# Reordering the load phase of a fused attention and gMLP kernel, and carrying waits to earlier matmuls

## The chip, the cores and the metric

The kernel runs on one core of one Trainium2 chip. The metric is the device time of one execution in microseconds. A kernel is run several times and the median is quoted. The chips and the executions differ by some microseconds (the kernel before took 866.45 us in the median of one call and 868.37 and 869.62 on another chip, its runs 865.66 to 870.82), so kernels are compared with the kernel before *of the same rounds on the same chip*. A ratio is the mean time of one kernel's fast runs over that of the other's of the same rounds, so it is not quite the ratio of the medians that stand beside it.

## The reference

A recurrent attention block (64 segments of 32 tokens; each segment sees 8 memory tokens that the one before produced) is followed by a gMLP block. Here only the start matters: the Q, K and V projections of tokens that do not depend on the recurrence.

```python
h = x + _A_ref(_layernorm(x), A_mem0, A_Wq, A_Wk, A_Wv, A_Wo, 32)   # x (1,2048,512), W (512,32,128)
# in _A_ref, for each of 64 segments:
h = concatenate([mem, xs]);  q, k, v = h@Wq, h@Wk, h@Wv
p = softmax(where(mask, q@k.T * scale, -1e9));  o = (p@v)@Wo
mem = o[:, :8];  outs.append(o[:, 8:])
# then
return h + _B_ref(_layernorm(h), B_w_in, B_w_sp, B_b_sp, B_w_out)
```

The projections of a segment's own 32 tokens do not depend on the memory tokens, and the kernel projects the last 8 tokens of every segment ahead, in chunks of 16 segments (128 tokens): chunks 0 and 1 in a *load phase* before segment 0, chunks 2 and 3 inside the segments.

## The kernel before

All engines' programs are written through an emitter that works out which semaphores each operation must wait for. A second wait of a matmul becomes an instruction of its own in PE's stream (221 semaphore instructions in the trace of the kernel before).

```python
def finalize(self):                       # (cut: dependencies -> waits, newest producer first)
    ...
            op.waits = waits
    ...
def emit(self, eng_name, eng, sems, dma_sems):
    for op in self.by_eng[eng_name]:
        for d in op.waits:
            ... eng.wait_ge(...)
        ins = op.fn(eng)
```

The loads, all from one queue (SP), in this order: the two x chunks (128 KB each), four Q weight pieces of 1 MB, three more x blocks. The V and K pieces (1 MB each, four of each) follow after the code below.

```python
    load_xe(0, 0)
    load_xe(1, 1)
    for hq in range(4):
        load_w(0, hq)
    load_x(0, 4); load_x(1, 5); load_xe(2, 6)          # (layout cut)
    ...
    def ln_stats(j):
        dve(bn_stats ...);  dve(bn_aggr ...)
        pool(tensor_scalar add EPS);  pool(tensor_tensor pow -0.5)      # (arguments cut)
    ...
    for j in range(2):
        ln_stats(j)
    for j in range(2):
        ln_apply(j)
        xT(j, 6 + j)            # four PE transposes
        xe_copy(j, 6 + j)       # one ACT copy of 128x512
```

The projection groups. A Q or K group is 16 matmuls of 128 columns (four heads), a V group 16 matmuls of 512 columns on quarter arrays; each goes to one of four PSUM banks in turn and is copied out by ACT or DVE. A V group's result goes to an SBUF buffer and from there to DRAM.

```python
    def vx_evac(ck, n, bank, eng="act"):
        if ck < 2:
            t, tok = part[:, n, :], [("part", n, 0), ("part", n, 1)]    # chunk 0 and chunk 1 share part[n]
        ...                                                           # copy to t, scaled
        sp(lambda e: e.dma_start(dst, ...t...), reads=tok, writes=[("vext", ck, n)])
    ...
    for i in range(8):                     # Q
        for ck in range(2): start_group(qkx_mm, qkx_evac, ck, i)
    for n in range(8):                     # V of chunk 0
        if n < 3: ln_apply(n + 4)
        start_v(0, n)
        if n == 1: xT(4, 6); ring_copy(0, 6)
        if n == 2: xT(5, 7); ring_copy(1, 7)
        if n == 3: xT(6, 6); xe_copy(2, 6); mem0_transpose(7); load_wo(0)
    load_wo(1)
    for j in range(2): load_vx(j)          # waits for chunk 0's stores
    for i in range(8, 12):  ...            # first half of K, both chunks
    for n in range(8):                     # V of chunk 1
        start_v(1, n)
        if n % 4 == 3: load_wo(2 + n // 4)
    for i in range(12, 16): ...            # second half of K
    # then the 64 segments
```

## Time and profile before

| | before |
|---|---|
| time, first rounds | 868.42 us (867.87 to 869.19) |
| profiled span | 866.1 us |
| PE busy | 849.6 us, 98% |
| first Q matmul | 7.82 us |
| Q groups end | 24.51 us |
| first half of K starts | 33.59 us |
| segment 0 starts | 55.12 us |

The page of the kernel before, its span and its busy rows (busy time of an engine, share of the span, instructions; then tenths of each of 40 slices):

```profile
span 866.1 us, 45456 instructions
PE 849.6 (98%) x22453; PEld 433.9 (50%) x18876; DVE 501.8 (58%) x1246; ACT 467.4 (54%) x1291; POOL 158.6 (18%) x427
PE   6999999999999999999999999999999999999998
DMA  9972232213141211222241313342211690032101
```

PE is the limit almost everywhere; only the first slice has room. DMA is full in the first two slices and most of the third, to about 60 us: that is the second limit of the load phase.

The timeline of the kernel before at its start (start in us, length in us, engine, line, operation, out<-in, shapes, count; in brackets the idle time before it and what ended that):

```profile
0.79 1.32 SPq L309 DMA_DIRECT2D f_xn<-in_A_x_dram  x2
2.16 2.69 SPq L315 DMA_DIRECT2D f_arena<-in_A_Wq_dram  x4
3.49 0.69 DVE L364 BATCH_NORM_STATS2 f_st<-f_xn 128x6 f32<-128x512 bf16 x1 [3.49 <-DMA f_xn<-in_A_x_dram]
5.40 0.41 DVE L374 TENSOR_SCALAR f_xn<-f_xn,f_mv,f_rs 128x512 bf16<-128x512 bf16 x1 [0.21 <-POOL f_rs L368]
7.82 16.37 PE L426 MATMUL f_ps<-f_hTe,f_arena 128*128 128x128 bf16 x249 [0.16 <-DMA f_arena<-in_A_Wq_dram]
```

The Q groups start when the first weight piece is there. By the records of the single matmuls, about 46 of them are 107 ns apart, until 12.7 us, and the rest 56 ns.

The PE timeline of the kernel before, the rest of the load phase:

```profile
24.51 1.91 PE L461 MATMUL f_ps<-f_arena,f_hTe 128*32 128x512 bf16 x32
26.90 0.40 PE L384 MATMUL f_ps<-f_ident,f_part 128*128 128x128 bf16 x4 [0.48 <-DVE f_part L374]
33.59 7.32 PE L426 MATMUL f_ps<-f_hTe,f_arena 128*128 128x128 bf16 x128
40.84 7.09 PE L461 MATMUL f_ps<-f_arena,f_hTe 128*32 128x512 bf16 x128
47.87 7.32 PE L426 MATMUL f_ps<-f_hTe,f_arena 128*128 128x128 bf16 x128
55.12 0.40 PE L280 MATMUL f_ps<-f_arena,f_hT 128*32 128x512 bf16 x4
```

From the first V group to segment 0, PE waits once, for 0.48 us.

### The profile page before, as it was taken

The numbers are of one execution on the slowest core, as the hardware profiler recorded it, in microseconds if no ns is written. First come the engines' busy times: TensorE is split into PE (matmuls) and PEld (weight loads), VectorE is DVE, ScalarE is ACT, GpSimd is POOL, SyncE is SP. The second block draws the span as 40 slices with busy tenths as digits, with TensorE's granted clock in tenths as the row PEclk, the third lists the DMA queues.
The fourth block names the chain that finished last, engine by engine and source line by source line (L and its number), as shares of the span: only waits on it lengthen the run. The fifth ranks groups of instructions, "written<-read, shape, count | busy, mean of one in ns | idle before, by whom it ended". The sixth has DMA issues, their size and how long they took to land.

```text
span 866.1 us, 45456 instructions
## 1 busy us (share of the span) xinstructions
PE 849.6 (98%) x22453; PEld 433.9 (50%) x18876; DVE 501.8 (58%) x1246; ACT 467.4 (54%) x1291; POOL 158.6 (18%) x427
## 2 busy tenths in 40 slices
PE   6999999999999999999999999999999999999998
PEld 6664445454445544455445554454554444444443
DVE  3446666666666666666666666566655564363343
ACT  3445666666666666666666666666666655400000
POOL 1621212121212212121211221121211122100000
PEclk9999999999999999999999999999999999999999
DMA  9972232213141211222241313342211690032101
GB/s 323 380 218 72 69 74 74 64 42 85 26 92 29 78 38 50 77 70 57 68 85 31 92 41 93 62 92 58 59 51 42 193 274 16 1 104 77 64 13 39
DMA packets 114180, 75.20 MB, mean 87 GB/s; under 512 B 70712, under 2 KB 99520, under 8 KB 113984
## 3 DMA queue, kind: packets, MB, share of 16 engines
q1 hardware_dynamic: 113840, 72.19, 30.4%
q8 instruction: 164, 2.69, 1.3%
q14 instruction: 32, 0.26, 0.1%
q10 hardware_dynamic: 144, 0.07, 0.0%
HBM read 39.46 MB, written 20.58 MB: 69 GB/s over the span
## 4 chain that ended last, share of the span: by engine, by line
PE 96%; DVE 2%; DMA 1%; issue 1%; SPq 0%; ACT 0%
PE f_ps L280 30%; PE f_ps L660 14%; PE f_ps L281 13%; PE f_ps L1092 11%; PE f_ps L426 3%; PE f_ps L710 3%; PE f_ps L461 3%; PE f_ps L1166 3%; PE f_ps L1054 3%; PE f_ps L574 3%; PE f_ps L1085 3%; PE f_ps L625 3%; PE f_ps L631 1%; PE f_ps L554 1%; PE f_ps L681 1%; DMA f_arena<-in_A_Wq_dram 1%
## 5 line engine op out<-in xcount | busy, mean ns | idle before, releaser
L280 PE MATMUL f_ps<-f_arena,f_hT 128*32 128x512 bf16 (+1 forms) x5120 | 352.8, 337 | 1.7 <-issue 0.5
L281 PE MATMUL f_ps<-f_arena,f_hT 128*32 128x256 bf16 (+1 forms) x3072 | 214.5, 308 | 0.0
L280 PEld LDWEIGHTS f_ps<-f_arena,f_hT 128*32 128x32 bf16 x5120 | 121.0, 96 | 168.8 <-issue 85.6
L518 ACT ACTIVATE f_Tst<-f_ps 128x512 bf16<-128x512 f32 (+1 forms) x320 | 149.9, 510 | 57.6 <-PE f_ps L280 53.9
L660 PE MATMUL f_ps<-f_arena,f_cT 128*32 128x256 bf16 x4096 | 134.6, 273 | 1.4 <-ACT f_cT L645 1.1
L597 POOL TENSOR_TENSOR f_E_sb<-f_R_sb,f_E_sb 128x64 bf16<-128x64 f32 x128 | 48.2, 377 | 378.5 <-ACT f_R_sb L589 378.5
L526 DVE STREAM_TRANSPOSE f_QT<-f_Tst 128x256 uint32<-128x256 uint32 x128 | 57.1, 446 | 94.9 <-ACT f_Tst L518 94.9
L660 PEld LDWEIGHTS f_ps<-f_arena,f_cT 128*32 128x32 bf16 x4096 | 92.7, 95 | 35.6 <-ACT f_cT L645 21.2
L1092 PE MATMUL f_ps<-f_arena 128*128 128x512 bf16 x448 | 100.6, 379 | 0.0
L617 DVE TENSOR_SCALAR f_V_sb<-f_ps 128x512 bf16<-128x512 f32 (+1 forms) x128 | 70.6, 551 | 41.1 <-PE f_ps L280 41.1
L672 ACT ACTIVATE f_part<-f_ps 128x256 bf16<-128x256 f32 x128 | 49.2, 384 | 68.2 <-PE f_ps L660 68.2
L647 DVE TENSOR_SCALAR f_cT<-f_ps 128x160 bf16<-128x160 f32 (+1 forms) x192 | 61.0, 373 | 38.0 <-PE f_ps L631 38.0
L645 ACT ACTIVATE f_cT<-f_ps 128x160 bf16<-128x160 f32 (+1 forms) x192 | 53.0, 348 | 38.9 <-PE f_ps L631 38.9
L1092 PEld LDWEIGHTS f_ps<-f_arena 128*128 128x128 bf16 x448 | 43.8, 98 | 52.7
L526 DVE STREAM_TRANSPOSE f_KT<-f_Tst 128x128 uint32<-128x128 uint32 (+1 forms) x192 | 66.0, 356 | 2.7
L585 ACT ACTIVATE f_R_sb<-f_ps 128x160 f32<-128x160 f32 x128 | 38.9, 304 | 33.5 <-PE f_ps L281 25.6
L1098 DVE TENSOR_TENSOR f_arena<-f_ps,f_arena 128x512 f32<-128x512 f32 x28 | 19.3, 689 | 54.4 <-PE f_ps L1092 52.4
L567 ACT ACTIVATE f_E_sb<-f_ps 128x224 bf16<-128x224 f32 x128 | 45.7, 357 | 0.1
L593 DVE TENSOR_TENSOR f_E_sb<-f_R_sb,f_E_sb 128x160 bf16<-128x160 f32 x128 | 44.7, 350 | 0.0
L589 ACT ACTIVATE f_R_sb<-f_R_sb 128x160 f32<-128x160 f32 x128 | 42.6, 333 | 2.0
L710 PE MATMUL f_ps<-f_arena,f_cTx 128*32 128x512 bf16 x512 | 40.6, 380 | 0.0
L280 PE MATMUL f_ps<-f_arena,f_hTe 128*32 128x512 bf16 x512 | 39.0, 382 | 0.0
(105 smaller groups left out, 1026.7 us busy)
## 6 DMA issues: line engine op xcount, KB each, us to landing
wT_d<-f_wst SPq DMA_DIRECT2D x32, 256.0 KB, 2.7
f_arena<-wT_d SPq DMA_DIRECT2D x32, 256.0 KB, 4.6
f_arena<-in_A_Wq_dram SPq DMA_DIRECT2D x4, 1024.0 KB
f_arena<-in_A_Wv_dram SPq DMA_DIRECT2D x4, 1024.0 KB
f_arena<-in_A_Wk_dram SPq DMA_DIRECT2D x4, 1024.0 KB, 16.0
f_arena<-in_A_Wo_dram SPq DMA_DIRECT2D x4, 1024.0 KB
f_Vx<-vext_d SPq DMA_DIRECT2D x128, 32.0 KB
f_xn<-in_A_x_dram SPq DMA_DIRECT2D x16, 128.0 KB, 2.7
```

The source lines that it names most:

```text
L280: return e.matmul(out, lhsT=lhsT, rhs=rhs, start=start, stop=stop, skip_group_check=True, tile_position=pos)
L281: return e.add_instruction(mybir.InstMatmult(name=nc.get_next_instruction_name(), engine=mybir.EngineType.PE, ins=[e.lower_ap(rhs), e.lowe ...
L518: act(lambda e: e.activation(out=st_.rearrange("p (hp i r) -> p hp i r", i=32, r=2), in_=ps[:, bank, 0:64 * np_].rearrange("p (hp r i) -> ...
L526: dve(lambda e: e.transpose(out=dst, in_=src), reads=tok, writes=[(nm, b, k) for k in halves(b, p0, np_)])
L597: pool(lambda e: e.tensor_tensor(out=ev, in0=rv, in1=ev, op=ALU.mult), reads=[("R", b), ("Ex", b)], writes=[("Ex", b)])
L617: dve(lambda e: e.tensor_scalar(out=dst, in0=src, scalar1=VSC, scalar2=None, op0=ALU.mult), reads=[PB(bank)], writes=tok)
L645: act(lambda e: e.activation(out=dst, in_=src, func=ACT.Copy, scale=UNSC), reads=[PB(PVB[c])], writes=tok)
L647: dve(lambda e: e.tensor_scalar(out=dst, in0=src, scalar1=UNSC, scalar2=None, op0=ALU.mult), reads=[PB(PVB[c])], writes=tok)
L660: pe(lambda e, h=h, g=g, i=i, b=b, c=c: e.matmul(ps[32 * g:32 * g + 32, bank, 0:d1 - d0], lhsT=cTh[:, i, 8:40], rhs=w_o[:, h, d0:d1], star ...
L672: act(lambda e: e.activation(out=part[:, s % 8, d0:d1], in_=ps[:, bank, 0:d1 - d0], func=ACT.Copy), reads=[PB(bank)], writes=[("part", s % ...
L710: pe(lambda e, h=h, g=g, i=8 * qr + bg: e.matmul(ps[32 * g:32 * g + 32, WXB, :], lhsT=cTx[:, rb % 2, i, :], rhs=w_o[:, h, :], start=(i < 4 ...
L1092: pe(lambda e: e.matmul(ps[:, bank, 0:TB], lhsT=z2[:, sc, fb * 128:(fb + 1) * 128], rhs=wTb[tb % 2][:, :, sc, :], start=(sc == 0), stop=(s ...
```

## The change

The intent is to start the Q groups sooner and with a warm array (the Q matmuls 56 ns apart from the first, not 107), to keep PE from running into the V and K weights, which come at the pace of DMA, and to rid PE of the separate wait instructions. The diff, cut to its core:

```diff
# finalize: a matmul's second wait is moved to the nearest earlier PE operation without one (at most 60 back, after the producer)
+        pe = self.by_eng["pe"]
+        for op in pe:
+            while len(op.waits) > 1:
+                d = op.waits[-1]
+                t = next((p for p in reversed(pe[max(0, op.pos - 60):op.pos]) if not p.waits and p.gidx > d.gidx), None)
+                if t is None:
+                    break
+                op.waits.pop()
+                t.waits = [d]
# loads: half a piece first; the second x chunk by ACT's queue
+        if mi == 0 and hq == 0:
+            cm = c0 + 4 * DH
+            sp(lambda e, c0=c0: e.dma_start(ws[:, :, c0:cm], wr[:, :, c0:cm]), writes=["W0"])
+            c0 = cm
+    load_xe(1, 1, "act")
     load_xe(0, 0)
-    load_xe(1, 1)
# chunk 1's first V groups get buffers of their own
-        if ck < 2:
+        if ck == 1 and n < 4:
+            t, tok = (hbuf, xo)[n // 2][:, n % 2, :], [(("h", "xo")[n // 2], n % 2)]
+        elif ck < 2:
# start: warming matmuls, 1/sqrt on ACT instead of POOL, copies in halves on ACT and DVE
-    for j in range(2):
-        ln_stats(j)
-    for j in range(2):
-        ln_apply(j)
-        xT(j, 6 + j)
-        xe_copy(j, 6 + j)
+    for _ in range(44):
+        pe(lambda e: e.matmul(ps[:, 1, 0:128], lhsT=onesrc[:, 0:128], rhs=onesrc[:, 0:128], start=True, stop=True), ...)
+    ln_bn(0)
+    ln_root(0)
+    ln_bn(1)
+    ln_apply(0)
+    ln_root(1)
+    xe_halves(0, 0, (6, 7))
+    ln_apply(1)
+    ...                               # first Q groups in halves, chunk 1's transposes between them
# V: half of chunk 1 between chunk 0's groups; the x transposes one V group of chunk 0 later
         start_v(0, n)
-        if n == 1:
+        if n % 2 == 1:
+            start_v(1, n // 2)
+        if n == 2:
             xT(4, 6)
...
-        if n == 3:
+        if n == 4:
             xT(6, 6)
             xe_copy(2, 6)
             mem0_transpose(7)
             load_wo(0)
...
-    for n in range(8):
+    for n in range(4, 8):
         start_v(1, n)
-        if n % 4 == 3:
-            load_wo(2 + n // 4)
+        if n % 2 == 1:
+            load_wo(n // 2)
```

More of the change, by code (lines that the diff above doesn't have):

```diff
@@ L305, in xbuf, with load_xe @@
         return (xn[:, j, :], [("xn", j)]) if j < 2 else (part[:, j, :], [("part", j, 0), ("part", j, 1)])
-    def load_xe(ck, j):
+    def load_xe(ck, j, q="sp"):
         t, tok = xbuf(j)
-        sp(lambda e: e.dma_start(t, xe[CK * ck:CK * ck + CK, XM:SEG, :]), writes=tok)
+        em.add(q, lambda e: e.dma_start(t, xe[CK * ck:CK * ck + CK, XM:SEG, :]), writes=tok, dma=True)
     def load_w(mi, hq):
@@ L314, in load_w @@
         c0, c1 = hq * 8 * DH, (hq + 1) * 8 * DH
+        if mi == 0 and hq == 0:
+            cm = c0 + 4 * DH
+            sp(lambda e, c0=c0: e.dma_start(ws[:, :, c0:cm], wr[:, :, c0:cm]), writes=["W0"])
+            em.mark_const("W0")
+            c0 = cm
         sp(lambda e: e.dma_start(ws[:, :, c0:c1], wr[:, :, c0:c1]), writes=[("W", mi, hq)])
         em.mark_const(("W", mi, hq))
+    load_xe(1, 1, "act")
     load_xe(0, 0)
-    load_xe(1, 1)
     for hq in range(4):
@@ L358, in late_consts, with ln_bn @@
         pool(lambda e: e.tensor_copy(out=mask[:, 224:448], in_=mask[:, 0:224]), reads=["mask"], writes=["mask"])
-    def ln_stats(j):
+    def ln_bn(j):
         t, tok = xbuf(j)
@@ L364, in ln_stats, with ln_root @@
         dve(lambda e: e.bn_stats(out=st1[:, k, :], in_=t), reads=tok, writes=[("st1", k)])
+    def ln_root(j):
+        k = j % 3
+        dve(lambda e: e.bn_aggr(out=mv1[:, k, :], in_=st1[:, k, :]), reads=[("st1", k)], writes=[("mv1", k)])
+        act(lambda e: e.activation(out=rs1[:, k:k + 1], in_=mv1[:, k, 1:2], func=ACT.Ln, bias=EPS), reads=[("mv1", k)], writes=[("rs1", k)])
+        act(lambda e: e.activation(out=rs1[:, k:k + 1], in_=rs1[:, k:k + 1], func=ACT.Exp, scale=-0.5), reads=[("rs1", k)], writes=[("rs1", k)])
+    def ln_stats(j):
+        k = j % 3
+        ln_bn(j)
         dve(lambda e: e.bn_aggr(out=mv1[:, k, :], in_=st1[:, k, :]), reads=[("st1", k)], writes=[("mv1", k)])
@@ L379, in ln_inplace, with xT @@
         ln_apply(j)
-    def xT(j, bank):
+    def xT(j, bank, dcs=range(DC)):
         t, tok = xbuf(j)
-        for dc in range(DC):
+        for dc in dcs:
             pe(lambda e, dc=dc: e.transpose(out=psb[:, bank, dc * 128:(dc + 1) * 128], in_=t[:, dc * 128:(dc + 1) * 128],
@@ L393, in x_flip @@
         sp(lambda e: e.dma_start(xs_d[i], t), reads=rd, writes=[("xs", i)])
-        sp(lambda e: e.dma_start_transpose(out=dst, in_=xs_d[i]), reads=[("xs", i)], writes=[tok])
+        sp(lambda e: e.dma_start_transpose(out=dst, in_=xs_d[i]), reads=[("xs", i)], writes=tok)
     def ring_fill(rb):
@@ L408, in xe_copy, with xe_halves @@
         src = psb[:, bank, 0:512].rearrange("p (dc c) -> p dc c", dc=DC)
-        act(lambda e: e.activation(out=hTe[:, ck % 3, :, :], in_=src, func=ACT.Copy), reads=[PB(bank)], writes=[("hTe", ck % 3)])
+        act(lambda e: e.activation(out=hTe[:, ck % 3, :, :], in_=src, func=ACT.Copy), reads=[PB(bank)],
+            writes=[("hTe", ck % 3, 0), ("hTe", ck % 3, 1)])
+    def xe_halves(ck, j, banks):
+        for hf in range(2):
+            xT(j, banks[hf], (2 * hf, 2 * hf + 1))
+        for hf in range(2):
+            src = psb[:, banks[hf], 256 * hf:256 * hf + 256].rearrange("p (dc c) -> p dc c", dc=2)
+            dst = hTe[:, ck, 2 * hf:2 * hf + 2, :]
+            if hf == 0:
+                act(lambda e, dst=dst, src=src: e.activation(out=dst, in_=src, func=ACT.Copy), reads=[PB(banks[0])], writes=[("hTe", ck, 0)])
+            else:
+                dve(lambda e, dst=dst, src=src: e.tensor_copy(out=dst, in_=src), reads=[PB(banks[1])], writes=[("hTe", ck, 1)])
     def mem0_transpose(bank):
@@ L417, in mem0_transpose, with qkx_mm @@
         act(lambda e: e.activation(out=hT[:, 0, :, 0:M], in_=src, func=ACT.Copy), reads=[PB(bank)], writes=[("hTm", 0, 0), ("hTm", 0, 1)])
-    def qkx_mm(ck, i, bank):
+    def qkx_mm(ck, i, bank, hhs=range(4)):
         mi, q = i // 8, i % 8
         ws = (w_q, w_k)[mi]
-        for hh in range(4):
+        for hh in hhs:
+            wt = "W0" if i < 2 and hh < 2 else ("W", mi, q // 2)
             h = 8 * (q // 2) + 2 * hh + q % 2
@@ L427, in qkx_mm @@
                                                          rhs=hTe[:, ck % 3, dc, :], start=(dc == 0), stop=(dc == DC - 1)),
-                   reads=[("hTe", ck % 3), ("W", mi, q // 2)], writes=[PB(bank)])
+                   reads=[("hTe", ck % 3, dc // 2), wt], writes=[PB(bank)])
     def qkx_evac(ck, i, bank, eng="act"):
@@ L445, in qkx_rows @@
                                           dc == 0, dc == DC - 1, (0, 32 * c)),
-               reads=[("hTe", ck % 3), ("W", mi, 2 * b), ("W", mi, 2 * b + 1)], writes=[PB(bank)])
+               reads=[("hTe", ck % 3, dc // 2), ("W", mi, 2 * b), ("W", mi, 2 * b + 1)], writes=[PB(bank)])
     def qkx_flip(ck, mi, r, b, bank):
@@ L462, in vx_mm @@
                                                        start=(dc == 0), stop=(dc == DC - 1), tile_position=(0, 32 * c)),
-                   reads=[("hTe", ck % 3), ("W", 2, n // 2)], writes=[PB(bank)])
+                   reads=[("hTe", ck % 3, dc // 2), ("W", 2, n // 2)], writes=[PB(bank)])
     def vx_evac(ck, n, bank, eng="act"):
-        if ck < 2:
+        if ck == 1 and n < 4:
+            t, tok = (hbuf, xo)[n // 2][:, n % 2, :], [(("h", "xo")[n // 2], n % 2)]
+        elif ck < 2:
             t, tok = part[:, n, :], [("part", n, 0), ("part", n, 1)]
@@ L758, in fast_path @@
     act(lambda e: e.preload_act_table_set("natural_log_exp_and_others"))
-    for j in range(2):
-        ln_stats(j)
-    for j in range(2):
-        ln_apply(j)
-        xT(j, 6 + j)
-        xe_copy(j, 6 + j)
+    for _ in range(44):
+        pe(lambda e: e.matmul(ps[:, 1, 0:128], lhsT=onesrc[:, 0:128], rhs=onesrc[:, 0:128], start=True, stop=True), reads=["onesrc"], writes=[PB(1)])
+    ln_bn(0)
[5 more added lines that the diff above has]
+    ln_apply(1)
+    for hp in range(2):
+        for i in range(2):
+            qkx_mm(0, i, 2 + i, (2 * hp, 2 * hp + 1))
+        if hp == 0:
+            xe_halves(1, 1, (0, 1))
+    qkx_evac(0, 0, 2, "act")
+    qkx_evac(0, 1, 3, "dve")
+    for i in range(2):
+        qkx_mm(1, i, 4 + i)
+        qkx_evac(1, i, 4 + i, ("act", "dve")[i])
     for mi in (2, 1):
@@ L785, in start_v @@
         start_group(vx_mm, vx_evac, ck, n)
-    for i in range(8):
+    for i in range(2, 8):
         for ck in range(2):
@@ L797, in fast_path @@
         start_v(0, n)
-        if n == 1:
+        if n % 2 == 1:
+            start_v(1, n // 2)
+        if n == 2:
             xT(4, 6)
             ring_copy(0, 6)
-        if n == 2:
+        if n == 3:
             xT(5, 7)
             ring_copy(1, 7)
-        if n == 3:
+        if n == 4:
             xT(6, 6)
@@ L985, in fast_path @@
         if j4 == 1 and 2 <= rb + 2 < RB:
-            late.append(lambda rb=rb: (ln_apply(0), x_flip(0, rb, xn[:, 1, :].rearrange("p (dc c) -> p dc c", dc=DC), ("xn", 1))))
+            late.append(lambda rb=rb: (ln_apply(0), x_flip(0, rb, xn[:, 1, :].rearrange("p (dc c) -> p dc c", dc=DC), [("xn", 1)])))
         if s == 2:
@@ L989, in fast_path @@
         if s == 3:
-            late.append(lambda: (ln_apply(7), x_flip(7, RB, hTe[:, 0, :, :], ("hTe", 0))))
+            late.append(lambda: (ln_apply(7), x_flip(7, RB, hTe[:, 0, :, :], [("hTe", 0, 0), ("hTe", 0, 1)])))
         if j4 == 1 and rb >= 2:
```

## The prediction

> **What bounds the kernel now.** The page gives PE 849.6 us busy of a span of 866.1 (98%), and the chain of work that ended last is 96% PE. From 60 to 640 us the table of stretches shows PE idle for under 0.6%. What can be had lies in the load phase, which ends where segment 0's matmuls start, at 55.12 us (timeline).
>
> Four losses, read from the timeline:
> 1. The first Q matmul starts at 7.82 us. The chain is: x lands about 3.47, statistics, two POOL operations (4.49 to 5.37), normalising (5.40 to 5.81), transposes, two 0.60 us ACT copies. It starts when the first 1 MB Q weight piece has landed (about 7.7).
> 2. Of the 256 Q matmuls the first 48 or so start 106.7 ns apart, until 12.7 us; then the spacing is 55.8 ns. That is 48 x 51 ns = 2.4 us. The granted-clock row doesn't show this. [...]
> 3. The first eight V groups take 24.51 to 33.59 = 9.08 us, where eight groups at 54 ns a matmul would take 6.9 and the 20 small transposes about 1.1. About 1 us is lost, 0.48 of it in a wait of the transposes for the normalising on DVE.
> 4. 219 separate semaphore instructions in PE's stream, two per segment.
>
> **What the change does.**
> - First piece 0.5 MB instead of 1 MB, issued 0.6 us earlier since the second x load goes by ACT's queue: it should land near 5.7 (1 MB takes 2.7 us in the trace).
> - Statistics by way of ACT instead of POOL, and copies in halves on ACT and DVE. The 44 warming matmuls, cold, take 44 x 0.107 = 4.7 us from about 1.1, so PE reaches the transposes near 5.5 to 5.8. I put the first Q matmul near 6.4: 1.4 us gained.
> - The array warm from there: 2.4 us gained, [...]less 0.3 for the second x chunk's transposes, now after the first Q groups.
> - V: the transposes come two groups later, so their wait goes: 0.5 to 0.7 us gained. Interleaving chunk 1 saves no work; it delays the need for K: PE 4 us earlier would want the first piece near 29.5, and it lands at 31.85 now.
> - Waits carried: around most of these instructions the spacing is the usual one; only in each segment's first value products is it 29 ns instead of 17: 64 x 12 ns = 0.8 us at most. I count 0.5.
>
> Sum: 1.4 + 2.4 - 0.5 + 0.6 + 0.5 = 4.4 us, all on PE's chain.
>
> **What could take it back.** The last output-projection weight piece lands at 61.9 and is first wanted soon after 63.1. PE comes some 4 us earlier; I estimate the piece at 58 to 60, with fewer stores ahead of it, so up to 1 us may be lost.
>
> **Predicted: 864.0 us, range 862.4 to 865.8.** Faster by over 2%: 0.01; within 2%: 0.98; slower: 0.01.
>
> **What would show it.** First Q matmul at 6.0 to 6.8; Q spacing 56 ns from the first or after at most a few; Q done near 21; first segment at 50.5 to 51.5 instead of 55.12; no PE wait for K or V weights; segments to the end shifted by the same 4 us, plus about 0.5.
>
> **What would make it wrong.** A cold spell after the warming matmuls; a PE wait for output weights in segment 0; carried waits that hold PE earlier than needed, or that are worth far more than the spacing suggests.

Its sum came to 4.4 us. A term of 0.2 us for the chance that the warm spell comes late, with the 0.3 us for the second chunk's transposes, makes up the 0.5 us that the sum takes off. That matmuls ahead of the Q groups would bring the 56 ns sooner was my estimate, from the one trace in which the spacing changed at 12.7 us, 4.9 us after the first Q matmul.

## The result

The changed kernel took 864.36 us in the median (863.59 to 865.12, 4 runs), the kernel before 868.14 us (867.4 to 869.19, 4 runs). The ratio is 0.9955 (95% interval 0.9938 to 0.9973). That is the predicted time within 0.4 us. Its parts are not the predicted ones, as the traces show.

The page of the changed kernel, the same rows:

```profile
span 862.4 us, 45321 instructions
PE 849.0 (98%) x22497; PEld 429.7 (50%) x18920; DVE 502.0 (58%) x1248; ACT 467.0 (54%) x1295; POOL 156.3 (18%) x423
PE   8999999999999999999999999999999999999998
DMA  9982322224141211332241413243221690032101
```

PE has 44 matmuls more, and 219 separate semaphore instructions less (221 before, 2 now, counted in the two traces).

The timeline of the changed kernel at its start:

```profile
1.08 4.82 PE L799 MATMUL f_ps<-f_onesrc 128*128 128x128 bf16 x44 [1.08 <-POOL f_onesrc L342]
1.54 0.82 SPq L326 DMA_DIRECT2D f_arena<-in_A_Wq_dram  x1
3.88 0.69 DVE L378 BATCH_NORM_STATS2 f_st<-f_xn 128x6 f32<-128x512 bf16 x1 [3.88 <-DMA f_xn<-in_A_x_dram]
5.77 0.34 PE L408 MATMUL f_ps<-f_ident,f_xn 128*128 128x128 bf16 x3
7.01 0.23 PE L408 MATMUL f_ps<-f_ident,f_xn 128*128 128x128 bf16 x1 [0.90 <-DMA f_arena<-in_A_Wq_dram]
7.62 0.95 PE L463 MATMUL f_ps<-f_hTe,f_arena 128*128 128x128 bf16 x14 [0.27 <-DVE f_hTe L445]
8.64 13.56 PE L463 MATMUL f_ps<-f_hTe,f_arena 128*128 128x128 bf16 x240
```

The small piece landed at 7.0 us, not at 5.7: half the bytes came only 0.7 us sooner. By the trace's records the 16 semaphore updates of the small piece came between 5.85 and 6.96 us, those of the 1 MB piece of the kernel before between 7.29 and 7.68. The fourth transpose, which waits for the small piece, started at 7.01 us, right after the last of them. By 5.8 us DMA had moved as many bytes of weights (0.53 MB) as the small piece has, by 6.96 us 0.93 MB: part of what it moved in between belonged to the pieces behind.

One sees here what a carried wait does: the Q groups' wait for their weights now stands on the fourth *transpose*, which has no need of weights. So the second half of the activations is copied only after the piece has landed, and the Q groups run steadily from 7.62 us, 0.2 us earlier than before. Apart from these waits the Q matmuls here are 56 ns apart from the first.

The timeline of the changed kernel, the rest of the load phase, PE with two evictions of chunk 1's V groups:

```profile
22.13 3.65 PE L498 MATMUL f_ps<-f_arena,f_hTe 128*32 128x512 bf16 x64
34.14 7.32 PE L463 MATMUL f_ps<-f_hTe,f_arena 128*128 128x128 bf16 x128
41.39 3.64 PE L498 MATMUL f_ps<-f_arena,f_hTe 128*32 128x512 bf16 x64
44.96 1.07 PE L463 MATMUL f_ps<-f_hTe,f_arena 128*128 128x128 bf16 x16
46.77 0.69 DVE L512 TENSOR_SCALAR f_part<-f_ps 128x512 bf16<-128x512 f32 x1 [4.54 <-DMA vext_d<-f_part]
47.51 1.68 PE L463 MATMUL f_ps<-f_hTe,f_arena 128*128 128x128 bf16 x27 [1.49 <-DVE f_part L512]
47.62 0.60 ACT L510 ACTIVATE f_part<-f_ps 128x512 bf16<-128x512 f32 x1 [3.90 <-DMA vext_d<-f_part]
53.87 0.40 PE L289 MATMUL f_ps<-f_arena,f_hT 128*32 128x512 bf16 x4
```

Here the expected gain goes. PE is 2.4 us ahead when the Q groups end (22.13 for 24.51). At the K groups it is 2.9 us ahead: 33.59 plus 3.46 us for the four V groups done early (64 matmuls of 54 ns), less 34.14. Then it waits 1.49 us at 47.5 us for a PSUM bank. The bank holds a V group of chunk 1 whose eviction (DVE, 46.77) waits for a *store*: `part[5]` still holds chunk 0's sixth V group, on its way to DRAM. By the landings in the trace, chunk 0's stores 5, 6 and 7 landed at 46.7, 47.5 and 47.8 us, right behind the first output-projection piece (1 MB, landed 46.2), which is issued ahead of them. Segment 0 starts at 53.87 us instead of 55.12: 1.25 us gained, not 3.9.

DMA had not become faster. By 20 us it had moved 6.31 MB in the kernel before and 6.09 MB in the changed one; by 48 us 16.46 and 16.17 MB.

The rest of the gain, from aligning the two traces matmul by matmul from the end: between segment 0 and 557 us the lead grows from 1.25 to 2.56 us, and between 557 and 575 us by another 1.35 us to 3.9, through two PE steps of 909 and 504 ns in the kernel before, without a wait on them.

### The profile page after: what moved, and what is told of

It reads as the page before. It is cut to its first block, busy times and chain, and to the rows that moved or that the text cites. A ratio compares the mean times of both kernels' runs of the same rounds, so it can differ in the third digit from the quotient of the medians.

```text
span 862.4 us, 45321 instructions
## 1 busy us (share of the span) xinstructions
PE 849.0 (98%) x22497; PEld 429.7 (50%) x18920; DVE 502.0 (58%) x1248; ACT 467.0 (54%) x1295; POOL 156.3 (18%) x423
## 3 DMA queue, kind: packets, MB, share of 16 engines
q8 instruction: 164, 2.69, 1.4%
## 4 chain that ended last, share of the span: by engine, by line
PE 96%; DVE 1%; DMA 1%; issue 1%; ACT 0%; SPq 0%; DVEq 0%
PE f_ps L289 30%; PE f_ps L699 14%; PE f_ps L290 13%; PE f_ps L1146 11%; PE f_ps L749 3%; PE f_ps L498 3%; PE f_ps L463 3%; PE f_ps L664 3%; PE f_ps L1220 3%; PE f_ps L1108 3%; PE f_ps L613 3%; PE f_ps L1139 3%; PE f_ps L593 1%; PE f_ps L670 1%; DMA vext_d<-f_part 1%; PE f_ps L720 1%
```

## The experiments

Twelve runs in three calls of four. The first call's chip was another than that of the second and third. All results were correct.

| run | median us | before us | ratio (95%) |
|---|---|---|---|
| carried waits taken out | 865.35 | 866.45 | 0.9992 (0.9978 to 1.0006) |
| carried after the Q groups only | 863.30 | 866.45 | 0.9960 (0.9947 to 0.9973) |
| output piece after the V stores | 862.79 | 866.45 | 0.9956 (0.9943 to 0.9969) |
| no interleaving | 864.38 | 866.45 | 0.9977 (0.9964 to 0.9989) |
| changed kernel, second call | 865.05 | 868.37 | 0.9960 (0.9947 to 0.9972) |
| before, with carried waits only | 867.08 | 868.37 | 0.9982 (0.9969 to 0.9995) |
| no warming | 868.65 | 868.37 | 0.9991 (0.9972 to 1.0010) |
| no warming, output piece later | 865.56 | 868.37 | 0.9968 (0.9953 to 0.9983) |
| changed kernel, third call | 865.30 | 869.62 | 0.9949 (0.9936 to 0.9962) |
| output piece after the V stores, again | 864.05 | 869.62 | 0.9930 (0.9915 to 0.9945) |
| the same with 20 bridging matmuls | 864.30 | 869.62 | 0.9941 (0.9927 to 0.9954) |
| first Q piece of 1 MB | 867.21 | 869.62 | 0.9972 (0.9959 to 0.9985) |

Three theories stood against each other for the load phase. The prediction's: PE's chain decides, so what the start gains arrives in the total. The second, from the trace: the landing of chunk 0's V stores puts a floor under the end of the phase. The third: DMA as a whole is the floor, and a wait taken away at one place comes back at another.

### The carried waits taken out

The block in `finalize` removed; everything else as changed.

```diff
-        pe = self.by_eng["pe"]
-        for op in pe:
-            while len(op.waits) > 1:
-                ...
```

> The changed kernel with each matmul's second wait put back as an instruction of its own. Theory of the prediction: carried waits are worth about 0.5 us in the segments, so 864.9 us. Theory from the two traces: they are worth about 23 ns in the median segment, 1.4 us over 63 segments, and at the start they cost 0.5 us, because the first weight piece's wait was carried onto the fourth transpose; but the start is made up at the wait near 47 us, which a transfer ends. So about 865.8 us, median segment 23 ns longer than in the changed kernel. Rival: the whole 2.6 us that the segments gained, with the two PE stalls near 561 and 570 us of the kernel before, come from them: 867 us, and the stalls are back at the same place.

The time, 865.35 us, lies between the two theories (864.9 and 865.8) and does not decide. Beside it, in the same call, stands the run of the next section, which differs only in that the waits after the Q groups are carried: 863.30 us, 2.05 less in the medians, and its slowest run (863.93) is below the fastest here (865.04). The median segment, counted from one ACT copy of the output projection to the next, was as long as in the kernel before and 22 ns longer than in the changed kernel's trace. The 561 us stalls did not come back at their place; this trace has one of 949 ns at 520 us, so such stalls wander. The Q groups did start at 6.51 us, but then PE waited 0.62 us for the second half piece, and the Q end (22.32) was no earlier: the start's cost that I had put on the carried wait is not shown.

### Carried after the Q groups only

```diff
-        for op in pe:
+        for op in pe[320:]:
```

The Q groups end at PE's 308th operation, so all their waits stay where they were.

> The changed kernel, but waits are carried only from PE's 321st operation on, so the first Q matmul waits for its weights itself. If the carried wait held the transposes back, the fourth transpose comes at about 5.8 us instead of 7.0 and the Q groups end about 0.5 us earlier (21.6 instead of 22.13). The time: if the wait of PE near 47 us is ended by a store's landing, it grows by that 0.5 us and the time stays at 864.4 (within 0.3). Rival: PE's chain is all that counts, and the time falls by 0.5 us.

The Q end was missed. The four transposes did come together at 5.71 us, but the piece landed at 7.0, the first Q matmul waited until 7.18, and 29 Q matmuls and the four transposes among them then ran at half rate: the groups ended at 23.41 us, 1.3 us *later* than in the changed kernel's first trace. Yet segment 0 started at 54.20, only 0.33 later, with the store wait shrunk to 0.56 us. The direction was not the one I had planned, but the floor of the second theory would absorb it in this way. The time, 863.30 us, missed the expected 864.4, which was taken from other rounds; the changed kernel did not run in this call, and the ratio (0.9960) is within what the changed kernel has elsewhere (0.9949 to 0.9960).

### The output piece after the V stores

One line moved: `load_wo(0)`, 1 MB, no longer between chunk 0's fifth and sixth V store.

```diff
             mem0_transpose(7)
-            load_wo(0)
+    load_wo(0)
     load_wo(1)
```

> The changed kernel with one line moved: the first output-projection weight piece (1 MB) is issued after the V groups' stores and no longer between the fifth and the sixth store of chunk 0. Theory: the 1.5 us wait near 47 us is a wait for the buffers of chunk 1's V groups 5 to 7, whose earlier contents leave behind that piece in the queue (2.7 us). Then those stores land before 45.2 instead of 46.7 to 47.8, the wait is under 0.3 us, segment 0 starts at 52.4 instead of 53.9, and the time is about 862.9. Rival: DMA as a whole is the limit, so the wait only moves, to the output weights in segment 0, and the time stays at 864.4.

> The run with the first output-projection piece after the V stores again, now beside the changed kernel. Segment 0 starts 1.5 to 2.2 us earlier than in the changed kernel. If the late instruction fetch in segment 0 is due to the load traffic, PE stalls there by 1 us or more and takes a part back: 0.8 to 1.6 us faster than the changed kernel. Without that stall: 1.5 to 2.2 us faster.

The "late instruction fetch" of the second text is my reading of the changed kernel's stop in segment 0 (at 60.42 us, 0.55 us without a wait, 1.46 us after a packet of the instruction queue had ended).

Both runs show the wait gone. The timeline of the second of them, the same two kinds of eviction and PE's K groups:

```profile
43.63 0.69 DVE L512 TENSOR_SCALAR f_part<-f_ps 128x512 bf16<-128x512 f32 x1 [1.12 <-PE f_ps L498]
44.49 0.60 ACT L510 ACTIVATE f_part<-f_ps 128x512 bf16<-128x512 f32 x1 [1.13 <-PE f_ps L498]
45.24 7.32 PE L463 MATMUL f_ps<-f_hTe,f_arena 128*128 128x128 bf16 x128
52.49 0.40 PE L289 MATMUL f_ps<-f_arena,f_hT 128*32 128x512 bf16 x4
```

The evictions now follow PE and not a store; the three stores landed at 42.7, 43.5 and 43.9 us. Segment 0 starts at 51.72 and 52.49 us in the two runs. In the third call this kernel took 864.05 us against 865.30 for the changed one, and each of its six runs (861.53 to 865.02) was below each of the five of the changed kernel (865.16 to 865.54). So it beats both kernels, by 1.25 us over the changed one in the medians, less than the 1.6 us that segment 0 is earlier. A part is lost in segment 0: PE stops there for 0.8 us in this trace and for 1.6 us in the first run's, without a wait on it (see "Late instructions" below). This speaks for the second theory; a share for the third is possible, but whether the load traffic causes these stops is not shown. Another way to take the floor away, buffers of their own for the other four V groups too, was not run.

### No interleaving

```diff
         start_v(0, n)
-        if n % 2 == 1:
-            start_v(1, n // 2)
...
-    for n in range(4, 8):
+    for n in range(8):
         start_v(1, n)
-        if n % 2 == 1:
-            load_wo(n // 2)
+        if n % 4 == 3:
+            load_wo(2 + n // 4)
```

> The changed kernel without the interleaving: all eight V groups of chunk 1 after the first half of K, as before. Theory of the prediction: PE then comes to K at about 30.2 and waits for its first piece until about 31.3, a wait of about 1 us; with the store wait near 45 us still there (about 1 us) the time is 864.4 to 865.2. Rival: the interleaving is worth nothing here, or costs (it puts three more stores ahead of those that PE waits for): 864.0 or below, and no K wait.

The PE timeline of this kernel has the K wait of the first theory (the wait stands on the last V matmul, again a carried one):

```profile
31.93 0.39 PE L498 MATMUL f_ps<-f_arena,f_hTe 128*32 128x512 bf16 x1 [0.80 <-DMA f_arena<-in_A_Wk_dram]
53.78 0.40 PE L289 MATMUL f_ps<-f_arena,f_hT 128*32 128x512 bf16 x4
```

There is no store wait on PE here. Segment 0 starts at 53.78 us, as early as with the interleaving (53.87). The time, 864.38 us, is at the lower edge of the first theory's range, whose store wait did not come. So the interleaving did remove the wait for K, and by the traces the changed kernel pays for it with the 1.5 us wait for stores, of which three more stand in front. That it is of use together with the later output piece is likely but not shown: no run has the later piece without the interleaving.

### The floor, in one table

All traces of kernels with the interleaving. "PE alone" is the Q end plus 30.06 us, which is what all four traces with the later output piece took from there, to 0.01 us (so their "lost" is 0 by definition; what counts is that the four agree).

| kernel | Q end | PE alone | segment 0 starts | lost |
|---|---|---|---|---|
| changed | 22.13 | 52.19 | 53.87 | 1.68 |
| changed, second call | 23.68 | 53.74 | 54.01 | 0.27 |
| changed, third call | 22.40 | 52.46 | 54.10 | 1.64 |
| carried waits out | 22.32 | 52.38 | 53.58 | 1.20 |
| carried later | 23.41 | 53.47 | 54.20 | 0.73 |
| no warming | 22.63 | 52.69 | 54.20 | 1.51 |
| piece of 1 MB | 24.08 | 54.14 | 54.30 | 0.16 |
| output piece later | 21.66 | 51.72 | 51.72 | 0 |
| output piece later, again | 22.43 | 52.49 | 52.49 | 0 |
| no warming, output piece later | 23.00 | 53.06 | 53.06 | 0 |
| bridging, output piece later | 22.35 | 52.41 | 52.41 | 0 |

With the early output piece the Q end moves by 2 us and segment 0 by 0.7. With the later one it moves one for one. That is the floor, shown: it goes when that one load is moved.

### The changed kernel again

The same kernel, beside the others.

> The changed kernel itself, as the reference for the other runs of this call. In the first pair of profiles 1.35 of the 3.9 us came from two PE stalls near 561 and 570 us of the kernel before that follow an instruction fetch. If they are chance, not the change, the gain here is about 2.5 to 3.5 us (ratio 0.996 to 0.997); if they belong to the kernel before, 3.8 us again (0.9955).

The two stalls end at 561.37 and 570.37 us; the packets of the instruction queue before them ended at 560.02 and 568.94.

> The changed kernel once more, as the reference for this call: ratio near 0.996; segment 0 starts at 53.8 to 54.1 us whether or not the array falls back to half clock before the Q groups.

The ratios were 0.9960 and 0.9949. The gain is thus 3.3 and 4.3 us of medians, on the same chip; the two do not settle whether the stalls near 561 and 570 us belong to the kernel before. The changed kernel's runs lie close (864.86 to 865.21 and 865.16 to 865.54), those of the kernel before far apart (866.48 to 869.92 and 868.12 to 870.82). This fits the floor, which hides the chances of the start; the kernel with the later output piece, without the floor, spreads too (861.53 to 865.02). The trace of the second call has such a chance. Its stretches, with PE's busy time first and the granted clock after POOL's column:

```profile
3.90:7.30 3.40, 1.61 (x26) 1.27 (x23) 1.77 (x5) 1.08 (x5) 0.00 (x0) 1.00 0.92 303
7.40:10.70 3.30, 3.08 (x30) 2.92 (x29) 0.91 (x3) 0.38 (x1) 0.00 (x0) 0.50 1.05 402
10.80:14.00 3.20, 3.20 (x61) 3.20 (x59) 1.46 (x2) 1.50 (x3) 0.00 (x0) 1.00 1.05 388
```

The array was warm from 3.9 us (26 matmuls in 1.61 us there, 27 in 2.80 before), but PE was busy for only 1.61 of the next 3.4 us, with a wait of 1.2 us for the weight piece. Then the clock stood at half for 3.41 us, and 24 Q matmuls and the four transposes among them ran at half rate. In the changed kernel's first trace PE was busy 2.23 of the corresponding 3.4 us, and the clock stayed. The Q groups ended 1.55 us later than there; segment 0 started 0.14 us later. By the records of the clock each of the four half-rate stretches that begin and end inside a trace is 3.41 us long.

### The carried waits alone

The block in `finalize` added to the kernel before, and nothing else.

> The kernel before with nothing but the carried waits. By the traces: 23 ns in the median segment, so 1.4 us faster than before (ratio 0.9984) and no change of the load phase. The prediction's size was 0.5 us (ratio 0.9994).

The ratio was 0.9982, 1.6 us: the size that the traces gave. The interval (0.9969 to 0.9995) still has room for the prediction's 0.5 us (0.9994); it is the traces that decide. From segment 0 to the end this trace took 809.52 us, 1.46 less than that of the kernel before. The median segment, counted as above, was 21 ns shorter, and 22 to 23 ns in the three traces of the changed kernel: over 63 segments 1.3 to 1.4 us. Counted from other marks it is 1 to 39 ns, so this size is rough. The place is firm: each segment has two groups of value products, and segment by segment the first takes 10 to 11 ns less and the second 39 to 43 ns less (medians) in each of the twelve traces with carried waits, and 0 ns less in the one that puts the instructions back. Other stretches give some of it back.

The load phase was expected not to change, but in this trace it did: the clock rose at 10.70 us instead of 12.69, and segment 0 started at 54.14 us, 0.98 earlier than in the trace of the kernel before and only 0.14 to 0.27 later than in the changed kernel's first two traces. It is the trace of this kernel's fastest run (865.47 of a median of 867.08). So the 1.25 us that the changed kernel gained in the load phase of the first pair is itself one draw.

### No warming

The 44 matmuls removed, from the changed kernel and from the one with the later output piece.

```diff
-    for _ in range(44):
-        pe(lambda e: e.matmul(ps[:, 1, 0:128], ...))
```

> The changed kernel without the 44 warming matmuls. Some 45 Q matmuls then start 107 ns apart instead of 56, and the Q groups end about 2.3 us later (near 24.4 us). If the load phase's end is set by the landing of chunk 0's stores, most is absorbed: the wait near 47 us (1.5 us) disappears, and the time is 0.7 to 1.0 us longer than the changed kernel's. Rival, PE's chain alone: 2.3 us longer.

> Both edits: no warming matmuls, and the first output-projection piece issued after the V stores. With the PE 2.3 us later there is no store wait left to remove, so this one equals the run without warming alone, within 0.4 us, that is 0.7 to 1.0 us longer than the changed kernel. If moving that piece is worth something of its own (1.5 us whatever PE does), it is shorter than the changed kernel.

Both expectations failed, and so the pair doesn't settle what the warming is worth. The Q end came at 22.63 and 23.00 us, not 24.4: the clock rose at 9.2 and 10.0 us here, where the kernel before had 12.7 in its trace. So the 2.4 us that I had read as the price of a cold start is one draw of several. With the warming the Q ends were 21.66 to 23.68 us, no clear difference. And the first kernel was 3.6 us slower than the changed one in the median, with runs at 865.2 and 866.2 and four at 868.3 to 869.5. All four slow runs have a mean clock of 0.997, the other two 0.999 and 1.000. The trace of one of the slow ones (869.04) shows what happened in it. Its stretches in segment 0:

```profile
60.40:63.80 3.40, 1.74 (x68) 0.90 (x60) 1.10 (x5) 1.08 (x5) 0.84 (x2) 1.00 0.31 92
63.90:67.20 3.30, 3.30 (x72) 2.17 (x64) 1.51 (x4) 0.69 (x3) 0.40 (x1) 0.50 0.21 55
```

and PE's timeline just before:

```profile
62.91 0.21 PE L664 MATMUL f_ps<-f_E_sb,f_V_sb 32*128 32x40 bf16 x5 [1.66 <-issue]
```

PE stopped for 1.66 us with no wait on it, was busy for 1.74 of the 3.40 us of the first row, and the clock stood at half (0.50) in the next 3.3 us. From segment 0's value products to segment 1's it took 12.9 us, with the stop in it, where the changed kernel's first trace has 9.7. Whether leaving out the 44 matmuls makes such stops longer is open. The second kernel's trace has a stop of the same length without the fall of the clock, and its median is 865.56 us.

### Twenty bridging matmuls

To the kernel with the later output piece, 20 more warming matmuls between the first transposes and the first Q matmul.

> The same with 20 more warming matmuls between the first transposes and the first Q matmul, while PE waits for the first weight piece. If idle PE before that piece lands is what drops the clock again in some runs, no half-clock window falls on the Q groups here, and they end at 21.7 to 22.4 us in the profile. As fast as the previous run or up to 0.7 us faster, with fewer slow executions. Rival: the extra matmuls only delay Q, 0.3 us slower.

The Q end (22.35 us) and the absence of a half-rate stretch over the Q groups were as expected in the one trace. The time, 864.30 against 864.05 us, was not better; without them the same kernel's trace was also free of such a stretch. Nothing gained that could be shown.

### The first Q piece of 1 MB

The split of the first piece undone.

> The changed kernel with the first Q weight piece at its old size (1 MB); everything else stays. The prediction put the small piece's landing 2 us before the old one; in the traces it lands at 6.2 to 7.2 us, where the old one landed at 7.6 to 7.7. So the piece should land at 7.1 to 7.7, the Q groups end up to 0.6 us later, and the store wait takes that up: the same time as the changed kernel, within 0.4 us.

The piece landed at 7.29 us, against 6.2 to 7.2 in the eleven traces with the small one. Segment 0 started at 54.30 us, 0.2 us after the changed kernel of this call, as expected. The time did not stay: 867.21 against 865.30 us. PE waited 1.29 us for the piece, the clock fell after that, and 28 Q matmuls and the four transposes among them ran at half rate (Q end 24.08), which the floor took up. The trace (866.53 us) is 1.0 us longer than that of the changed kernel in this call: 0.2 us at segment 0, 0.7 us by a stop of PE in segment 0 (60.78 us, without a wait), and little on balance after that. Two other runs (867.54 and 868.13) had a mean clock of 0.995 (one half-rate stretch of 3.41 us is 3.41 x 0.5 / 866 = 0.002), so there was at least one such stretch more in them, and where it fell no trace tells. So the small piece is worth something here, 1.9 us, and not by an earlier start; by what, stays open.

### Late instructions

In the traces, PE steps of over 430 ns without any wait, from segment 0 on, end 1.3 to 2.0 us after the end of a packet of the *instruction* queue (a row of its own on the page: 164 packets, 2.69 MB in the kernel before; all 25 such steps with an idle time of over 150 ns before them, up to the end of the segments; the packets come some 4 us apart there, so by chance about one step in six would). The two of the kernel before at 561.37 and 570.37 us follow packets that ended at 560.02 and 568.94; the changed kernel's stop in segment 0 (60.42 us) follows one that ended at 58.96. Such a packet is 16 KB and takes 1.01 us at the median in the trace of the kernel before, 1.11 in that of the changed one. In the segments (70 to 640 us) they come 255 PE instructions apart on average in both traces, matmuls and weight loads counted from start to start; around segment 0, while the loads fill DMA, the gap grew to 329 (changed), 370 (changed, second call), 368 (output piece later, first run) and 465 instructions (no warming). The gap alone doesn't tell: the kernel before has one of 350 there and no such stop. So I read these stops as PE running out of instructions because the fetch came late under the load traffic. No run took the traffic away to test it, so the cause is argued from the times and not shown by experiment.

## Why the prediction was right or wrong

The time was right, but by luck in part. The load phase was to give 3.9 us (1.4 + 2.4 - 0.5 + 0.6) and gave 1.25 in the first pair of traces. The carried waits gave about 1 us more than their 0.5, which makes up less than half of what was missing. The rest of that pair's 3.9 us came from two stalls in the trace of the kernel before. Point by point, as the prediction put it:

- "First piece 0.5 MB instead of 1 MB [...] should land near 5.7": wrong, and this is the first step to fail. It landed at 7.0, at 6.2 to 7.2 in all traces. The bytes came as fast as I had assumed (0.53 MB of weights by 5.8 us), but the transpose that waits for the piece started only after the last of its 16 updates (6.96 us; 7.01). In the eleven traces the parts of the small piece are spread over 0.9 to 2.1 us, those of a 1 MB first piece over 0.4 to 0.6 (three traces). Why they are spread so is open. "First Q matmul near 6.4: 1.4 us gained": 7.07, and steady from 7.62, so 0.2 us.
- "The array warm from there: 2.4 us gained": held in the first trace, where no Q matmul was at half rate, but that the warming earned it is not shown: without it the cold spell ended at 9.2 and 10.0 us, not at 12.7. And in the eight traces with warming and the small piece (bridging left out) the clock fell again in two, after PE had waited 1.2 us (changed, second call) and 1.07 us (carried later) for the piece; I had set aside 0.2 us for a late warm spell, an estimate without a trace behind it. And the clock row did show such a fall (0.50 from 7.4 to 10.7 us in the second call's trace); only the cold start itself it left out (1.00 from 7.8 to 12.6 us in the kernel before, with the Q matmuls 107 ns apart).
- "V: [...] 0.5 to 0.7 us gained": held, 2.9 less 2.4 us.
- "All on PE's chain": wrong, and the largest step to fail. PE reached K 2.9 us ahead and segment 0 only 1.25. I had checked the weights' landings against PE's times, and the stores' not: I did not see that chunk 1's evictions wait for chunk 0's stores, and that the output piece stands before them. The run with that piece moved shows it.
- "What could take it back: [...] the last output-projection weight piece": PE did not wait for it in segment 0 of the changed kernel. It stopped there for another reason, by my reading instructions that came late.
- "Waits carried: [...] 64 x 12 ns = 0.8 us at most. I count 0.5": too small by a factor of two to three. I had taken one spacing (29 for 17 ns) for the cost. A spacing of 29 ns, after the first four value products, is still there in the changed trace; what became shorter are the ends of the two groups, by some 10 and 40 ns. Alone the carried waits gained 1.6 us (ratio 0.9982).
- Of the 3.9 us by which the aligned traces differ, 1.25 are the load phase, 1.3 the segments, and 1.35 two stalls in the trace of the kernel before, which I read as late instructions. In the later calls the gain was 3.3 and 4.3 us all the same. I have one trace of the kernel before, so how often its longer start and its stalls occur stays open; the one other trace with its load phase (the carried waits alone) reached segment 0 0.98 us sooner.

## What to carry to other kernels

When a phase is bound by one engine and loads fill DMA beside it, lay PE's *new* times beside every landing that it or an eviction needs, the stores that free a buffer included; a large load queued before a small store can put a floor under the phase, and moving that one load was worth 1.25 us here, where more warming matmuls showed no gain. A wait carried to an earlier instruction saved time in the segments here (1.6 us by the carried waits alone), but it can also hold back work that did not need it, as the fourth transpose was, so look where it came to stand. Test a start-up gain at the end of the phase, not where it arises.

## What the traces leave open

- What lets the clock fall. In the first two traces the clock's records change twice each, at 12.69 and 866.03 us and at 5.70 and 862.45 us: 853.33 and 856.75 us apart, 250 and 251 times 3.413. Counted in stretches of 3.41 us from the changes of the clock, four in which PE was still busy 1.53 to 1.75 us were followed by a fall (two are shown above); one with 1.94 us (changed kernel, third call, from 46.15 us) was not, and neither was one with only 1.59 us (second call, from 857.25 us, near the end). So the busy time alone does not draw the line.
- A single stop of 1.66 us for no wait that the profile shows stood before such a fall too (no warming, 62.91 us); the stop and the fall together made that segment 3.2 us longer than in the changed kernel's first trace.
- The traces have PE stops of 0.5 to 1.9 us that end 1.3 to 2.0 us after an instruction packet has ended, the longest of them in segment 0, beside the loads; that these stops are late fetches is inferred.
- What one separate semaphore instruction costs in PE's stream is not measured. Taking 219 of them out gave 1.6 us (ratio 0.9982, 0.9969 to 0.9995), and the one spacing that the prediction went by (12 ns a segment) understated it.
